# Delta-rule attention and a gelu MLP in one kernel: another list for the order of all five engines

## The chip, the cores and the metric

The kernel runs on one core of a Trainium2 chip. The core has a matmul engine (TensorE, PE in the profile; its weight loads are listed as PEld), a vector engine (VectorE, DVE), an engine for activation functions (ScalarE, ACT), a general engine (GpSimd, POOL), and SyncE (SP), which here only issues DMAs. ACT and POOL issue some DMAs too. Each engine works through its own row of instructions in order; waits between engines are waits on semaphores. PE reads operands from SBUF and writes into PSUM, which has eight banks.

The metric is the device time of one execution in microseconds (us); less is better.

## The reference

Two computations in a row. First a delta-rule attention over 4 batches, 8 heads, 768 positions and a head size of 48:

```python
k_n = k / (np.linalg.norm(k, axis=-1, keepdims=True) + 1e-06)
state = zeros((B, H, D, D))
for t in range(S):
    y[:, :, t] = einsum('bhd,bhde->bhe', q[:, :, t], state)
    v_old = einsum('bhde,bhd->bhe', state, k_n[:, :, t])
    state = state + beta_t * einsum('bhd,bhe->bhde', k_n[:, :, t], v[:, :, t] - v_old)
```

Its output, 3072 tokens of 384 numbers (8 heads of 48), goes through an MLP: `h = x @ w_in` (384 to 2048), gelu in its tanh form, `g @ w_out` (2048 to 384).

## The kernel before

**Attention.** The 768 positions are cut into 12 chunks of 64, c0 to c11. All 32 batch-head pairs are worked on together. Within a chunk the recurrence becomes matrices of 64 by 64: the keys of a chunk are normalized (`sq`, the square; `ss`, its sum; `sr` and `nw`, the root by two ways; `rn`, the reciprocal; `Kn`, the normalized keys), the keys and queries are turned by PE (`KQT` holds the result), products of keys with keys are formed (the "own" products of 32 by 32 blocks, and `G`, `Tt`, `DT` from the larger ones), a triangular system is solved, and from the solution come the factors (`Yf`, `tmp`, `XW`, `TB`, `WB`, `DI`, `ET`, `TT`) of an inverse. With it the chunk's `R` (values less what the state predicts), `U` (the solved values), the new state `S` and the output `x` are made. State follows state: c1 needs c0's.

Chunks 0 and 1 are solved singly: chunk 0's solve runs on DVE (lines 799 to 832), chunk 1's on POOL. From chunk 2 on they are solved in pairs, on POOL: 28 short instructions on `Yf` and `tmp` (L790, L793) between the transposition `Tt` on DVE that opens the solve (L904) and `XW` that ends it (L840, L846). Copies of `TB` by DMA (SP's queue) and expansions (`WB`, `DI`, L1024) follow, then PE's inverse.

The norm of chunks 0 to 5 takes its root on ACT; that of c6 to c11 is computed without ACT's root, by three rounds of short instructions that go to and fro between DVE and POOL (L633 to L644, the parts marked `norms(..., True)` on POOL), for two chunks at once.

**MLP.** Tokens come in 8 tiles: t0 to t3 are chunks 0 to 3 (64 positions of 4 batches, so 256 columns), t4 to t7 are two chunks each (512 columns). The first layer (`x,W` in the profile) has 16 blocks of 128, each followed by gelu on ACT (`gT`); the second (`W,gT`) sums over them and is copied out through `osb`.

**Order.** The program first records every operation with its reads and writes (`Plan.op`), and numbers it. Nothing is planned at build time beyond that: `Plan.schedule` (lines 137 to 166) reads a long string, `ORDER`, from left to right. A token is a letter for the engine (p, v, a, g, s for PE, DVE, ACT, POOL, SP) and the number of an operation; each engine's row is its tokens in that order. So a token can also say on which engine an operation runs, where several can do it. A token `wK.B` is K matmuls on a constant of zeros, `wz`, into bank B of PSUM (`spin`, line 415; the matmuls appear as L418 with `ps<-wz`): they compute nothing that is used. A second string, `BANK`, gives the PSUM bank of every result of PE. `Plan.emit` then puts the waits: an operation waits for what it reads, for the readers of what it overwrites, and for the last users of the bank that it takes.

## Time and profile before

| | |
|---|---|
| three runs | 244.82 us median (242.86 to 246.46) |
| profiled execution | 245.22 us |
| its span, from first to last instruction | 243.4 us |
| mean granted clock of PE | 0.958 of full |
| busy: PE, PEld, DVE, ACT, POOL | 221.4, 149.5, 157.4, 148.9, 123.3 us |

The span is what the profiler sees between the first and the last instruction; the 1.8 us between it and the execution's time lie around it. PE is busy for 91% of the span. PE's busy time counts the matmuls on the constant, and a matmul at half clock counts with its longer duration. In the rows of a timeline, the first number is the start in us from the span's start, the second the length, then engine, line, operation, what is written from what is read, and the count; in brackets stands how long the engine had been idle and what ended that. Line numbers are those of the kernel before; the changed kernel has one line more at the head, so that all of its numbers below are higher by one.

### The profile page before, as it was taken

The numbers are of one execution on the slowest core, as the hardware profiler recorded it, in microseconds if no ns is written. First come the engines' busy times: TensorE is split into PE (matmuls) and PEld (weight loads), VectorE is DVE, ScalarE is ACT, GpSimd is POOL, SyncE is SP. The second block draws the span as 40 slices with busy tenths as digits, with TensorE's granted clock in tenths as the row PEclk, the third lists the DMA queues.
The fourth block names the chain that finished last, engine by engine and source line by source line (L and its number), as shares of the span: only waits on it lengthen the run. The fifth ranks groups of instructions, "written<-read, shape, count | busy, mean of one in ns | idle before, by whom it ended". The sixth has DMA issues, their size and how long they took to land.

```text
span 243.4 us, 11359 instructions
## 1 busy us (share of the span) xinstructions
PE 221.4 (91%) x5084; PEld 149.5 (61%) x5102; DVE 157.4 (65%) x317; ACT 148.9 (61%) x295; POOL 123.3 (51%) x261
## 2 busy tenths in 40 slices
PE   7778867978896999999997999998899999999995
PEld 4354546767575976878874676565556656555562
DVE  6689984969797558985998988688736562000000
ACT  2247833688787477954976788735596437635502
POOL 4249897698588861888736886568700000000000
PEclk9999965799999589999999999999999999999999
DMA  6999999999645334575226311352032311200113
GB/s 140 180 156 162 187 198 131 198 180 159 114 86 112 81 74 98 97 163 97 41 67 159 67 37 38 73 101 74 3 62 59 60 39 47 72 33 32 64 35 129
DMA packets 64785, 23.78 MB, mean 98 GB/s; under 512 B 53600, under 2 KB 63840, under 8 KB 64736
## 3 DMA queue, kind: packets, MB, share of 16 engines
q1 hardware_dynamic: 57952, 14.66, 34.7%
q10 hardware_dynamic: 5728, 5.25, 7.5%
q0 software_dynamic: 1056, 3.15, 7.5%
q8 instruction: 40, 0.66, 1.2%
q14 instruction: 9, 0.07, 0.1%
HBM read 20.64 MB, written 4.72 MB: 104 GB/s over the span
## 4 chain that ended last, share of the span: by engine, by line
PE 59%; DMA 13%; ACT 8%; DVE 7%; SPq 4%; POOL 3%; issue 3%; ACTq 1%
PE ps L268 57%; DMA kf<-in_k_dram 12%; SPq L276 4%; ACT G L261 2%; DMA x<-x 1%; DVE TT L1131 1%; ACTq L276 1%; PE ps L663 1%; ACT gT L261 1%; DVE DT L750 1%; ACT sq L261 1%; ACT ET L1090 1%; POOL tmp L790 1%; ACT Tt L740 1%; POOL Yf L793 1%
## 5 line engine op out<-in xcount | busy, mean ns | idle before, releaser
L268 PE MATMUL ps<-x,W 128*128 128x256 bf16 (+1 forms) x369 | 68.9, 335 | 3.8 <-issue 1.4
L261 ACT ACTIVATE gT<-ps 128x512 bf16<-128x512 f32 x96 | 53.2, 605 | 30.0 <-PE ps L268 28.1
L268 PE MATMUL ps<-W,gT 128*128 128x384 bf16 x384 | 67.3, 327 | 0.2 <-issue 0.2
L268 PEld LDWEIGHTS ps<-x,W 128*128 128x128 bf16 x384 | 41.2, 117 | 21.6 <-DVE DT L750 2.1
L268 PEld LDWEIGHTS ps<-W,gT 128*128 128x128 bf16 x384 | 35.9, 98 | 23.3 <-issue 0.3
L793 POOL TENSOR_TENSOR Yf<-Yf,tmp 128x28 f32<-128x28 f32 (+13 forms) x84 | 30.2, 360 | 6.4
L790 POOL TENSOR_TENSOR tmp<-Yf 128x28 f32<-128x28 f32 (+13 forms) x84 | 30.1, 359 | 5.9
L257 DVE COPY osb<-ps 128x384 f32<-128x384 f32 x8 | 4.4, 554 | 29.5 <-PE ps L268 29.5
L1131 DVE TENSOR_TENSOR TT<-ps,DI 64x384 bf16<-64x384 f32 (+5 forms) x36 | 15.2, 422 | 7.1 <-PE ps L268 6.7
L1024 POOL TENSOR_TENSOR DI<-TB,mB 128x384 bf16<-128x384 bf16 x12 | 11.0, 933 | 16.3 <-DMA TB<-TB 13.8
L750 DVE TENSOR_TENSOR DT<-ps,mD 128x512 bf16<-128x512 f32 x24 | 15.9, 683 | 4.8 <-ACT G L261 4.8
L418 PE MATMUL ps<-wz 128*128 128x512 bf16 x69 | 17.1, 402 | 1.7 <-DVE pat L425 1.3
L261 ACT ACTIVATE osb<-ps 128x384 f32<-128x384 f32 x16 | 7.7, 488 | 16.5 <-PE ps L268 13.7
L252 DVE TENSOR_TENSOR TT<-ps,DI 128x768 bf16<-128x768 f32 (+2 forms) x18 | 12.1, 684 | 8.7 <-PE ps L268 8.6
L261 ACT ACTIVATE G<-ps 128x512 bf16<-128x512 f32 x24 | 13.6, 592 | 2.4 <-DVE Tt L742 1.4
L261 ACT ACTIVATE x<-ps 128x1024 bf16<-128x1024 f32 (+3 forms) x14 | 11.3, 824 | 5.6 <-PE ps L268 5.6
L268 PE MATMUL ps<-KQT 48*64 48x128 bf16 (+1 forms) x640 | 11.9, 208 | 2.9 <-ACT KQT L261 1.4
L261 ACT ACTIVATE sq<-kf 128x768 f32<-128x768 f32 (+1 forms) x11 | 8.9, 813 | 8.4 <-DMA kf<-in_k_dram 8.3
L611 DVE TENSOR_REDUCE ss<-sq 128x16 f32<-128x768 f32 (+1 forms) x13 | 11.3, 879 | 3.3 <-ACT sq L261 3.3
L268 PEld LDWEIGHTS ps<-TT,ET 64*64 64x64 bf16 x640 | 10.3, 113 | 4.4 <-issue 1.5
L418 PEld LDWEIGHTS ps<-wz 128*128 128x128 bf16 x72 | 7.1, 103 | 9.4 <-DVE pat L425 1.3
L268 PEld LDWEIGHTS ps<-KQT 48*64 48x64 bf16 (+1 forms) x640 | 8.7, 101 | 6.2 <-ACT KQT L261 2.3
(146 smaller groups left out, 363.7 us busy)
## 6 DMA issues: line engine op xcount, KB each, us to landing
qf<-in_q_dram SPq DMA_DIRECT2D x24, 192.0 KB, 4.5
kf<-in_k_dram SPq DMA_DIRECT2D x23, 192.0 KB, 5.6
vf<-in_v_dram SPq DMA_DIRECT2D x40, 96.0 KB, 3.3
out_dram<-osb ACTq DMA_DIRECT2D x16, 192.0 KB, 2.1
W<-in_moe_w_out_dram POOLq DMA_DIRECT2D x4, 384.0 KB, 8.9
out_dram<-osb ACTq DMA_DIRECT2D x16, 96.0 KB, 3.1
vf<-in_v_dram SPq DMA_DIRECT2D x4, 192.0 KB, 5.8
W<-in_moe_w_in_dram POOLq DMA_DIRECT2D x2, 384.0 KB, 9.5
```

The source lines that it names most:

```text
L252: return lambda e: e.tensor_tensor(out() if callable(out) else out, a() if callable(a) else a, b() if callable(b) else b, op)
L257: return lambda e: e.tensor_copy(out, a() if callable(a) else a)
L261: return lambda e: e.activation(out, a() if callable(a) else a, func)
L268: ins = t.matmul(out, lhsT, rhs, start=st, stop=sp_, skip_group_check=skip)
L276: return lambda e: e.dma_start(out, a)
L418: ins = e.matmul(psum[:, b, :], wz[:, 0:128], wz[:, :], start=True, stop=True)
L611: fr = lambda e, u=u: e.tensor_reduce(ss[j][:, u], sq[:, u, :], AX.X, ALU.add)
L750: op(d_ps(512), {"dve": lambda e: e.tensor_tensor(dv, gview(1)(), md, ALU.mult)}, reads=[h] + MD, writes=[dn])
L790: sop(nb * s * w, lambda e, s=s, w=w, tv=tv: e.tensor_tensor(tv, yf[:, :, s:s + 1, 0:s].to_broadcast([128, nb, w, s]), Yv()[:, :, s + 1:16 ...
L793: sop(nb * s * w, lambda e, s=s, tv=tv: e.tensor_tensor(Yv()[:, :, s + 1:16, 0:s], Yv()[:, :, s + 1:16, 0:s], tv, ALU.add), [YN, TN], [YN])
L1024: return e.tensor_tensor(o_.rearrange("q p (b j) -> q p b j", j=16), i_.unsqueeze(2).to_broadcast([128, n_, 3, 16]), mB[:, 16 - 16 * w:64 ...
L1131: ins = e.tensor_tensor(TT[r_][o_, par::2, cols], bank(hk, par)[i_, 0:8 * n].rearrange("q (p t) -> q p t", t=n), DI[r_][o_, par::2, 16 * k ...
```

## The change

Both strings are replaced as a whole; nothing else is touched. All operations are the same, apart from the matmuls on the constant: six tokens with 72 such matmuls became one with five. The table itself tells a reader nothing, so that only these pieces are shown:

```diff
 ORDER = """
-v0 g11 s52 a53 g21 v37 v5 v49 w6.0 g22 a51 s50 g16 v6 g18 v8 v38 v44 g13 v4 v1 s57 a2 g14 g12 g19 v15 s58 v48 g20 v39
...
+g405 w5.3 g406 v254 s119 g407 s118 a221 g35 v304 s116 g408 s117 g409 p314 s114 g410 a378 g411 p231 s266 a309 g412 v379
...
-BANK = ("06035030223020716021312502331474655413667456202312530375435460212600502436647540243530466307732633"
+BANK = ("0070325215530761467526743765467223026600550166045677331475733026221446304255770173061702204601200627"
```

What this does to the rows is shown at three places. The first is the start. PE's first row before, in which `wz` marks the matmuls on the constant, `Kn` the turning of keys, `KQT 32x32` an own product of a chunk and `DI`, `WB` the inverse of chunk 0:

```order
L418 MATMUL ps<-wz 128x512 x6
L268 MATMUL ps<-identF,gT 128x128 x3
L418 MATMUL ps<-wz 128x512 x22
L695 MATMUL ps<-identB,Kn 128x128 x8
L268 MATMUL ps<-KQT 32x32 x64
L418 MATMUL ps<-wz 128x512 x12
L663 MATMUL ps<-identB,Qn 128x4x2x16 x16
L695 MATMUL ps<-identB,Kn 128x128 x8
L268 MATMUL ps<-KQT 32x32 x64
L268 MATMUL ps<-KQT 64x128 x32
L418 MATMUL ps<-wz 128x512 x29
L268 MATMUL ps<-R,TT 64x48 x16
```

and PE's row now, from the same place on:

```order
L269 MATMUL ps<-identF,gT 128x128 x3
L696 MATMUL ps<-identB,Kn 128x128 x8
L269 MATMUL ps<-KQT 32x32 x64
L696 MATMUL ps<-identB,Kn 128x128 x8
L269 MATMUL ps<-KQT 32x32 x64
L664 MATMUL ps<-identB,Qn 128x4x2x16 x16
L269 MATMUL ps<-KQT 64x128 x32
L269 MATMUL ps<-TT,G 64x48 x32
L269 MATMUL ps<-R,TT 64x48 x16
L696 MATMUL ps<-identB,Kn 128x128 x16
L269 MATMUL ps<-DI,ET 64x48 x16
L269 MATMUL ps<-KQT 32x32 x64
```

The constant's matmuls are gone from here; the five that are left stand ahead of the first state product of chunk 1 and of the MLP's first group. The keys of chunks 2 and 3 are turned earlier (`Kn`, 16 matmuls), and the own products of these two chunks, which stood behind chunk 0's state, stand inside chunk 0's inverse.

The second place is ACT. Its row near the start before, where `warm` is a one-element root whose only use is to bring a table of functions in early:

```order
L261 ACT_TABLE_LOAD
L261 ACTIVATE warm<-warm 128x1
L261 ACTIVATE sq<-kf 128x384
L455 ACTIVATE mF<-me 64x48
L261 ACTIVATE sr<-ss 128x16
```

and now:

```order
L262 ACT_TABLE_LOAD
L262 ACTIVATE sq<-kf 128x384
L262 ACT_TABLE_LOAD
L262 ACTIVATE warm<-warm 128x1
L262 ACTIVATE sr<-ss 128x16
```

The square of chunk 0's first half has moved ahead of `warm`, and the program has a third load of a table (the other one stands ahead of the first gelu in both). Further down in ACT's row the square of chunk 4's keys, which before stood between the copies of the inverse of chunk 0 (`WB`) and its `U`, stands behind chunk 0's `S` and ahead of the last copy of `x`; on DVE its sum moves likewise. DVE takes chunk 1's `Kn` from POOL and does it ahead of chunk 0's solve, has two sums inside that solve where it had one, and has the `Kn` of chunks 2 and 3 ahead of the first `ET` of chunk 0's factors. Two copies of `KQT` that stood inside that solve are ACT's now.

The third place is the solve of chunks 6 and 7. DVE's row before, from the last part of the key products (`Tt1`) on; `Tt0` is the transposition that opens the solve, `rn` the reciprocal of the norms of chunks 8 and 9, `Kn2` the keys of chunk 8:

```order
L742 SCALAR_TENSOR_TENSOR Tt1<-ps,mH,Tt1 128x2x128
L750 TENSOR_TENSOR DT3<-ps,mD 128x2x4x64 x2
L904 STREAM_TRANSPOSE Tt0<-Tt1 128x1024
L637 SCALAR_TENSOR_TENSOR nw<-nw,sr 128x32
L638 SCALAR_TENSOR_TENSOR sr<-nw,sr 128x32
L252 TENSOR_TENSOR TT1<-ps,DI1 128x16x48
L252 TENSOR_TENSOR S0<-ps,S1 128x16x48
L257 COPY KQT2<-ps 128x2x4x128
L257 COPY KQT3<-ps 128x2x4x128
L252 TENSOR_TENSOR R0<-ps,vf1 128x768
L252 TENSOR_TENSOR ET1<-ps,mE 128x2x8x48
L252 TENSOR_TENSOR TT1<-ps,DI1 128x16x32
```

and now, where `rn` stands ahead of the last two parts of `Tt1` and of `Tt0`:

```order
L638 SCALAR_TENSOR_TENSOR nw<-nw,sr 128x32
L639 SCALAR_TENSOR_TENSOR sr<-nw,sr 128x32
L751 TENSOR_TENSOR DT3<-ps,mD 128x2x4x64
L751 TENSOR_TENSOR DT2<-ps,mD 128x2x4x64
L642 TENSOR_SCALAR nw<-nw 128x32
L645 RECIPROCAL rn<-nw 128x32
L736 TENSOR_SCALAR Tt1<-ps,mH 128x2x128
L743 SCALAR_TENSOR_TENSOR Tt1<-ps,mH,Tt1 128x2x128
L905 STREAM_TRANSPOSE Tt0<-Tt1 128x1024
```

POOL's row ahead of the same solve, whose first instruction is `Yf0<-Tt0,bM0`, before:

```order
L1024 TENSOR_TENSOR DI1<-TB0,mB 128x8x48
L257 CAST Qn<-qf 128x2x8x48
L1024 TENSOR_TENSOR DI1<-TB0,mB 128x8x48
L1024 TENSOR_TENSOR DI2<-TB0,mB 128x8x48
L257 CAST Qn<-qf 128x2x8x48
L252 TENSOR_TENSOR nw<-sr,ss 128x32
L252 TENSOR_TENSOR bM0<-nbT,mS 128x512
L252 TENSOR_TENSOR nw<-sr,ss 128x32
L252 TENSOR_TENSOR Yf0<-Tt0,bM0 128x512
```

and now:

```order
L1025 TENSOR_TENSOR DI2<-TB0,mB 128x8x48
L253 TENSOR_TENSOR nw<-sr,ss 128x32 x2
L1025 TENSOR_TENSOR DI1<-TB0,mB 128x8x48 x2
L253 TENSOR_TENSOR nw<-sr,ss 128x32 x2
L258 CAST Qn<-qf 128x2x8x48 x2
L253 TENSOR_TENSOR Kn3<-kf0,rn 128x16x48
L253 TENSOR_TENSOR Kn2<-kf2,rn 128x16x48
L253 TENSOR_TENSOR Yf0<-Tt0,bM0 128x512
```

Two `Kn` that were DVE's are POOL's here, ahead of the solve, and the last two steps `nw` of the norm stand behind all expansions `DI` of chunks 4 and 5's factors. On PE the first product that needs this solve's result (`WB` of chunk 7) stands some ten operations earlier in its row.

More of the change, by code (lines that the diff above doesn't have):

```diff
@@ L76 @@
[L76 to L81 removed]
+s52 v45 a53 g13 v48 g11 g16 s50 v4 a51 v36 v37 v5 g18 s55 g12 g21 v15 g14 s54 g19 g20 g22 p64 s57 v66 s59 v8 v49 a85
@@ new lines @@
+p599 a597 s261 p244 v600 g813 v598 a601 v572 p341 a602 g214 p452 p342 a337 a453 v573 v603 p343 g574 a245 p344 g456
+v454 p345 p441 v575 g439 a346 v347 p604 a442 v576 p609 v605 g577 p356 g614 v578 v579 a606 v610 p360 s226 v580 v611
+a607 p364 g457 v581 a612 v582 v615 p248 a514 g515 s524 s525 p249 a361 g583 v608 s223 a357 g616 a365 v613 s225 p443
+a584 a458 v585 p459 g617 v444 a250 s522 p362 g618 a460 s224 g619 p366 v586 g620 p339 a367 p445 g621 v340 a440 g622
+p587 s593 a689 g623 v446 p467 g624 p461 a363 v468 g625 p447 a588 g626 g627 p354 v448 v462 g628 p469 a355 g629 p352
```

111 lines of the change are left out of this document (53 added, 58 removed).

## The prediction

> **What bounds the kernel now.** I read the page of the profile first, then its windows by stage, then the chain of waits, and last the timelines of single engines.
>
> ```profile
> span 243.4 us, 11359 instructions
> PEclk9999965799999589999999999999999999999999
> L418 PE MATMUL ps<-wz 128*128 128x512 bf16 x69 | 17.1, 402 | 1.7 <-DVE pat L425 1.3
> ...
> 20.00:42.60 22.60, 17.73 (x467) 11.87 (x458) 17.78 (x40) 12.90 (x33) 19.41 (x45) 0.78 1.08 171
> 42.60:60.00 17.40, 15.29 (x330) 12.36 (x332) 14.49 (x23) 13.88 (x28) 14.35 (x30) 0.90 1.07 178
> 60.00:80.00 20.00, 17.22 (x494) 13.06 (x495) 16.25 (x34) 15.41 (x35) 15.54 (x31) 1.00 0.60 113
> 80.00:88.00 8.00, 8.00 (x226) 6.72 (x223) 3.49 (x6) 4.41 (x6) 6.92 (x18) 0.57 0.19 39
> 80.30:87.10 6.80, 6.80 (x212) 5.85 (x212) 3.19 (x6) 3.85 (x5) 5.72 (x17) 0.50 0.18 35
> 88.00:122.00 34.00, 33.67 (x956) 26.21 (x956) 28.55 (x50) 24.56 (x46) 21.89 (x42) 1.00 0.52 102
> 133.00:202.00 69.00, 66.16 (x1985) 42.53 (x1993) 49.59 (x90) 44.67 (x84) 31.91 (x71) 1.00 0.26 56
> 202.00:243.40 41.40, 38.20 (x216) 21.63 (x209) 2.90 (x4) 18.11 (x34) 0.00 (x0) 1.00 0.18 61
> ```
>
> The rows of windows give the stretch, its length, and the busy time of PE, PEld, DVE, ACT and POOL, then the clock. There are two regimes. From 88 us on PE is busy for nearly the whole stretch (33.67 of 34.00, 66.16 of 69.00): nothing but fewer or shorter PE instructions, or a new wait, changes the time there. Before 88 us there is slack: PE idles 2.1 us in 42.6 to 60 and 2.8 us in 60 to 80, and ran 6.8 us from 80.3 at a clock of 0.50. Before 42.6 us 17.1 us of its busy time are matmuls on the constant, so PE waits for the chain of chunk 0 there:
>
> ```profile
> 15.80 1.57 POOL Kn L252
> ...
> 18.03 15.39 DMA kf<-in_k_dram
> 33.45 0.85 ACT sq L261
> 34.32 0.95 DVE ss L611
> 35.27 0.60 DVE DT L750
> 35.87 0.60 DVE KQT L257
> 36.47 0.47 DVE U L257
> ```
>
> Each row is start, length, what. A load of k for a later chunk lands at 33.4; its square stands ahead of chunk 0's work in ACT's row, its sum in DVE's, so chunk 0's U comes only at 36.47.
>
> **The first 45 us.** The numbers needed:
>
> ```profile
> 2.15 1.28 ACT L261 ACT_TABLE_LOAD   x1 [2.15 <-issue]
> 7.89 0.52 ACT L261 ACTIVATE sq<-kf 128x384 f32<-128x384 f32 x1 [4.25 <-DMA kf<-in_k_dram]
> 9.50 0.22 ACT L261 ACTIVATE sr<-ss 128x16 f32<-128x16 f32 x1 [0.95 <-DVE ss L611]
> 22.74 0.95 DVE L611 TENSOR_REDUCE ss<-sq 128x16 f32<-128x768 f32 x1
> 31.84 1.01 DVE L252 TENSOR_TENSOR Kn<-kf,rn 128x768 bf16<-128x768 f32 x1
> 12.90 0.65 PE L268 MATMUL ps<-KQT 48*32 48x32 bf16 x64 [1.15 <-ACT KQT L261]
> 36.99 0.53 PE L268 MATMUL ps<-U,Kn 64*48 64x48 bf16 x32 [2.02 <-DVE U L257]
> 41.09 1.36 PE L268 MATMUL ps<-KQT 48*32 48x32 bf16 x128
> 42.44 1.44 PE L268 MATMUL ps<-x,W 128*128 128x256 bf16 x6
> 74.75 1.50 PE L268 MATMUL ps<-x,W 128*128 128x256 bf16 x12
> ```
>
> *Constant matmuls removed.* 67 of 72 go. Each group stood in a gap in which PE had to wait for chunk 0, so I take 0 for their time. What they held up is the clock: it was full from 5 to 32.5 us. That is worth little there: 64 small matmuls took 0.65 us at full clock (12.90), 128 took 1.36 at half (41.09). For the MLP's large ones it is worth nearly half (1.44 us for six at 42.44, 1.50 for twelve at 74.75), but the clock was at half when these began, spins or not. Cost 0, bounds 0 and 2 (eighteen large ones more at half clock, 0.115 each).
>
> The Trainium skill, "TensorE: Matmul & The Clock Gate", Part 1, says that the clock falls to half after an idle window of about 3.4 us, whatever ran before, and rises after one busy window. By that rule five matmuls just ahead of the MLP warm nothing and the first MLP groups run at half clock, as they did in this trace; it would leave the sum as it is unless gaps between those groups come back, which is a rival below.
>
> *Second table load.* The row now has sq ahead of warm, with a load before each. The first falls into the wait for k; the second begins when sq ends: 8.41 + 1.28 + 0.20 for warm = 9.89, where sr began at 9.50: +0.4 us. Other reordered rows around it (the sum and the beta transposition on DVE) I put at up to 0.6; the first own product moves from 12.9 to 13.9: +1.0.
>
> The Trainium skill, "ScalarE: Activation LUTs", section "What ACT_TABLE_LOAD costs", puts a drain of about 1.4 us on every switch of set beside 1.28 us of load. The load's 1.28 is in this trace; no row shows a drain. With it, this step would be an estimated +1.8 in place of +0.4.
>
> *DVE and ACT ahead of chunk 0's factors.* DVE takes chunk 1's Kn from POOL (1.57 there, 1.01 here), ahead of the solve of chunk 0: +1.0. Two sums instead of one stand inside that solve: +0.95. Two Kn of chunks 2 and 3 stand ahead of the factors' ET: +2.0. Two KQT copies leave that stretch for ACT: -1.2. One square (0.85) now stands on ACT ahead of the last copy of x, which gives the MLP its input: +0.85. And the square and sum that held up U are behind it: PE's wait of 2.02 us at 36.99 goes. Sum with the start: 1.0 + 1.0 + 0.95 + 2.0 + 0.85 - 1.2 - 2.0 = **+2.6**: the first MLP group at 45.0 instead of 42.4. Bounds: -1 (the additions fill gaps of DVE, which is busy 17.78 of 22.60 us) and +6 (the copies hold ACT up too).
>
> **From 45 to 88 us.** What waits here are the states of chunks 2 and 3, whose solve as a pair on POOL is late:
>
> ```profile
> 42.52 1.25 DVE L904 STREAM_TRANSPOSE Tt<-ps 128x1024 f32<-128x1024 f32 x1 [1.47 <-PE ps L268]
> 62.49 1.21 POOL L846 TENSOR_TENSOR XW<-Yf,nbT 128x256 bf16<-128x256 f32 x2
> 79.08 0.24 PE L268 MATMUL ps<-DI,ET 64*64 64x48 bf16 x4 [1.02 <-issue]
> ```
>
> The own products of chunks 2 and 3 stand now ahead of chunk 0's inverse on PE, not behind its state, and the transposition that opens the solve can run at about 37 us instead of 42.5. POOL still has chunk 1's solve to end, so I take 4 us earlier; two casts of Q (0.8 each) move out of it too, and XW is done at about 57, not 63.7. Then the inverses and states of this pair need not be waited for: PE's slack of 2.1 + 2.8 us and the cold stretch can go. At half clock 6.8 us cost between 0 (all small matmuls) and 3.4 (all large); the stretch is mixed: 2.0. Sum 6.9, of which I leave 0.3 for a Q cast that now comes late: **-6.6**, bounds 0 and -8. So at 88 us PE is ahead by 6.6 - 2.6 = 4.0 us.
>
> **From 88 to 133 us.** This lead meets the solve of chunks 6 and 7:
>
> ```profile
> 100.89 1.97 DVE L904 STREAM_TRANSPOSE Tt<-Tt 128x1024 f32<-128x1024 f32 x1
> 103.24 0.26 POOL L252 TENSOR_TENSOR nw<-sr,ss 128x32 f32<-128x32 f32 x1 [0.66 <-DVE sr L638]
> 103.45 1.28 POOL L252 TENSOR_TENSOR Yf<-Tt,bM 128x512 f32<-128x512 f32 x1
> 109.45 0.34 DVE L644 RECIPROCAL rn<-nw 128x32 f32<-128x32 f32 x1
> 119.21 1.21 POOL L846 TENSOR_TENSOR XW<-Yf,nbT 128x256 bf16<-128x256 f32 x2
> 121.87 0.84 PE L268 MATMUL ps<-x,W 128*128 128x256 bf16 x6
> 122.75 0.53 DVE L1024 TENSOR_TENSOR WB<-TB,mB 128x768 bf16<-128x768 bf16 x1
> 129.11 0.44 PE L268 MATMUL ps<-WB,G 64*64 64x48 bf16 x32
> 132.20 1.24 PE L268 MATMUL ps<-x,W 128*128 128x512 bf16 x5 [1.25 <-ACT ET L1090]
> ```
>
> From Tt at 100.89 to WB of chunk 7, ready at 123.3, runs an unbroken chain of POOL: 17 us. Before, PE asked for chunk 7's WB at 129.1, long after. The new list asks earlier: what stands ahead of that product now had been done in this trace at about 121.5, and with a lead of 4.0 PE is there at 117.5. The solve cannot move up as far. In DVE's row the reciprocal rn of chunks 8 and 9, at 109.45 in this trace and behind Tt, now stands ahead of Tt, and on POOL two Kn of these chunks (1.57 each by the row at 15.80) stand ahead of Yf; the two Kn run beside Tt and its last addends (some 3.2 us), so they cost nothing if rn comes in time. With all of it I put Tt, and so WB, at 2.1 us earlier than before: 121.2. PE then waits 3.7 us, and the lead left is **-0.3**. Bounds: WB as late as now, 123.3, makes +1.8; a WB that keeps step with PE makes -4.0.
>
> **After that.** The wait at 132.2 stays: in SP's row the moves of x for the next tile now stand some 1.5 us later behind TB's copies, but PE has just waited, so 0, bounds -1.2 and +1.5. From 133 us the same matmuls are in another order behind one another; PE's 2.8 us of idle there, and 3.2 in the last stretch, most of it the tail, I leave: 0, bounds -2 and +1.
>
> **Sum.** +2.6 - 6.6 + 3.7 + 0 = -0.3 against the profiled run of 245.22 us (span 243.4, 1.8 outside it): 244.9. That run lies 0.4 over the median of 244.82, so the time to expect is **244.5 us**.
>
> **Rivals.**
>
> *Faster: the lead survives.* If pair 6 and 7 keeps step (bound -4.0) and half of the later start isn't there (1.3 less), the profiled run becomes 245.2 - 5.3 = 239.9 and the median 239.5; with all of it, 238.2. For it speaks that before 88 us PE has the 6.9 us of slack worked out above, and that all of the start's additions lie on DVE and ACT, which had gaps. Against it: the 17 us of solve that don't shrink, and a list in which PE wants their result 10 operations sooner. The windows from 88 us on say that a lead is kept only if no wait is put into PE's work; here one is.
>
> *Slower: rn holds up Tt.* The norm of chunks 8 and 9 goes to and fro between DVE and POOL; its last POOL step ended at 103.5, and on POOL it stands now behind two expansions of DI, which wait for a copy of TB by DMA. If that step comes no earlier than 103.5, then rn (0.34), two parts of Tt and the transposition of 1.97 end at about 107, WB at 127, and PE, due at 121.5 without a lead, has lost 5.5: 250.7 in the profiled run, 250.3 as a median. It decides from the point where the last nw is later than about 102. Against it: the copies of TB for chunks 4 and 5 come earlier when PE is ahead.
>
> *Slower: the MLP stays at half clock.* If PE's gaps after 45 us come back at each group, the 48 matmuls of the first tile's first layer cost 0.24 us instead of 0.125 each. That is 5.5 us, of which this trace already pays 2.0 for its first eighteen: 3.5 more than in the sum, 248.0, within 2%.
>
> *No change at all.* From 88 us PE does the same work. If gains and losses ahead of it cancel, the time is as before, 244.8; my sum is nearly that case, and I count it there.
>
> **Chances.** About 2% is what a measurement of this kernel can tell from no change: 239.9 and 249.7. My forecast with its near neighbours (no change; the half-clock MLP, most of it) 0.51; the lead surviving 0.26; rn or a start 6 us later, unrecovered (251 at worst), 0.23. So faster 0.26, same 0.51, slower 0.23. The range reaches into both rivals: from 238.2, the whole lead, to 250.3; the likeliest case alone spans 241 to 248.
>
> **What would show it.** Right: the ACT row shows two loads ahead of sr, and sr at about 9.9; the first x,W group at 44 to 47 us; XW of pair 2 and 3 at about 57; no half clock at 80 to 87; PE some 4 us ahead at 88 and a wait of 2 to 5 us for WB of chunk 7 near 118. Wrong: no such wait (then faster), the last nw of chunks 8 and 9 after 102 us (then slower), or a start later than 48.

## The result, and the profile after

The changed kernel takes **264.81 us** (median of four runs, 264.23 to 265.19); the kernel before, run beside it, 245.05. The ratio is 1.081 (95% interval 1.073 to 1.090): slower by 8%, outside the forecast range of 238.2 to 250.3. Ratios here leave out executions that are 1.5% or more longer than the fastest of their kernel, medians don't.

The runs below were made in five further sets, each with the kernel before beside it; its median went from 242.4 to 245.6 us from set to set. Kernels of different sets are therefore compared by their ratios to the kernel before, and a difference of 2 or 3 us between their times alone says little.

The page of the changed kernel, its span and two rows of its 40 slices (busy tenths of PE, granted clock):

```profile
span 262.8 us, 11239 instructions
...
PE   2132475698988789798979899999997989999995
...
PEclk9999999999999977999999999999999999999999
```

Windows of the changed kernel (stretch, length, busy PE, PEld, DVE, ACT, POOL, then the clock):

```profile
20.00:42.60 22.60, 11.63 (x329) 9.44 (x329) 15.69 (x40) 13.21 (x32) 18.81 (x44) 1.00 1.13 177
42.60:60.00 17.40, 13.09 (x238) 9.57 (x239) 9.54 (x15) 11.53 (x27) 13.84 (x35) 1.00 0.53 78
88.00:122.00 34.00, 29.00 (x791) 23.15 (x791) 24.79 (x42) 19.66 (x35) 20.91 (x42) 0.90 0.43 87
133.00:202.00 69.00, 66.40 (x1612) 41.58 (x1603) 49.59 (x89) 45.06 (x84) 36.56 (x77) 1.00 0.32 68
```

PE issued 329 matmuls in 20 to 42.6 us where it had issued 467, and idled 5.0 of the 34 us from 88 us on, where it had idled 0.33. The clock of 1.00 in the first rows is not to be trusted: the clock was first recorded at 57.2 us, and the matmuls ahead of it have the pace of half clock (of the 18 `x,W` at 54.06 below, the first 15 start 0.21 us apart, the last 0.11).

The waits of PE in the changed kernel (what waited, for whom, us in total, times, longest):

```profile
PE ps L269 <- issue: 9.3, 8, 2.3
PE ps L696 <- DVE Kn L253: 7.6, 2, 5.9
PE ps L269 <- DMA x<-x: 4.8, 4, 1.5
PE ps L664 <- ACT Qn L262: 4.6, 1, 4.6
```

The same view of the kernel before begins with this row:

```profile
PE ps L268 <- issue: 2.9, 11, 1.0
```

"issue" is time in which PE waited for nothing that the profile shows. Nine of the eleven stops of before, 0.15 to 0.18 us each and 1.5 us together, lie inside rows of large matmuls; that trace holds 5084 matmuls for 5102 weight loads, so these are most likely matmuls whose records are missing. The changed kernel's trace holds 5035 of both and has no such stops. Without them, and with a stop of 1.0 us that the view lists under L696, PE stopped for 1.3 us before (two stops) and for 10.3 us now (nine). The timeline of the changed kernel has the other places:

```profile
6.45 1.28 ACT L262 ACT_TABLE_LOAD   x1 [6.45 <-DMA kf<-in_k_dram]
7.74 0.52 ACT L262 ACTIVATE sq<-kf 128x384 f32<-128x384 f32 x1
8.28 1.28 ACT L262 ACT_TABLE_LOAD   x1
9.58 0.20 ACT L262 ACTIVATE warm<-warm 128x1 f32<-128x1 f32 x1
9.69 0.20 ACT L262 ACTIVATE sr<-ss 128x16 f32<-128x16 f32 x1
...
13.67 1.25 POOL L253 TENSOR_TENSOR bM<-btz,mS 128x512 f32<-128x512 f32 x1 [5.28 <-DVE btz L253]
13.79 1.96 DVE L253 TENSOR_TENSOR Kn<-kf,rn 128x768 bf16<-128x768 f32 x1
...
28.12 0.63 DVE L838 STREAM_TRANSPOSE TB<-XW 128x256 f32<-128x256 f32 x1
...
38.07 0.41 PE L269 MATMUL ps<-R,TT 64*64 64x48 bf16 x7 [1.82 <-issue]
44.54 0.53 PE L269 MATMUL ps<-KQT 48*64 48x128 bf16 x11 [2.30 <-issue]
...
51.26 2.31 PE L419 MATMUL ps<-wz 128*128 128x512 bf16 x5 [1.18 <-DVE osb L1224]
54.06 3.68 PE L269 MATMUL ps<-x,W 128*128 128x256 bf16 x18
```

Chunk 0 is solved (`TB`) 3.0 us later than before (25.13), the first MLP group begins at 54.06, 11.6 us later. From there to the end of one group of tile 2's first layer, which the trace puts at 104.4 us before and at 116.7 now, the distance is nearly the same. From that group to the span's end it is 146.1 against 139.0: another 7.1 us. So some 12 of the 19.4 us are lost ahead of the MLP, 7 in its second half, nothing between. In that second half PE waits 3.3 us for x and stops for 2.8 us at "issue", where it was 0.5 and 0.3 before.

**Where the "issue" stops lie.** The DMA view lists a queue of the kind "instruction". From its records and the rows of matmuls, I counted the matmul at which each of these stops lies:

```
kernel    packet of 16384 bytes: asked, ended   PE stopped ... went on   at matmul no.
before            76.43   77.82                  78.05 ... 79.08          1493 = 11*128 + 85
after             35.62   36.60                  36.25 ... 38.07           351 =  2*128 + 95
after             41.44   43.02                  42.24 ... 44.54           479 =  3*128 + 95
after             90.69   91.64                  91.29 ... 92.96          1498 = 11*128 + 90
after            130.39  131.50                 131.45 ... 132.85         2519 = 19*128 + 87
```

They lie whole multiples of 128 matmuls apart (the remainder falls slowly, since PE's row holds 34 semaphore instructions too and before's trace lacks 18 matmuls), and each ends 1.3 to 1.5 us after a packet has. I call these places marks. PE went on 2.3 to 3.1 us after the packet had been asked for, and it had been asked for only 0.6 to 1.6 us before PE stopped; what sets the moment of the asking is not shown. 128 matmuls and their 128 weight loads are 256 instructions. The Trainium skill, "Runtime: NRT & Kernel Launch", section "Instruction fetch mechanics", says that an engine's instructions come in blocks of 16 KiB, which are 256 instructions, and that crossing a block's end is mostly hidden. The first half agrees with these records; the second does not agree with stops of up to 2.3 us.

### The profile page after: what moved, and what is told of

Same layout as the page of the kernel before. It is cut to its first block, busy times and chain, and to the rows that moved or that the text cites. A ratio compares the mean times of both kernels' runs of the same rounds, so it can differ in the third digit from the quotient of the medians.

```text
span 262.8 us, 11239 instructions
## 1 busy us (share of the span) xinstructions
PE 214.7 (82%) x5035; PEld 146.8 (56%) x5035; DVE 165.5 (63%) x312; ACT 154.3 (59%) x302; POOL 121.3 (46%) x260
## 4 chain that ended last, share of the span: by engine, by line
PE 58%; DVE 12%; ACT 9%; DMA 7%; SPq 6%; issue 6%; ACTq 0%
PE ps L269 55%; SPq L277 6%; DMA x<-x 4%; DMA kf<-in_k_dram 2%; DVE Kn L253 2%; PE ps L664 1%; DMA TB<-TB 1%; ACT KQT L262 1%; PE ps L696 1%; ACT L262 1%; ACT x L262 1%; PE ps L419 1%; ACT Qn L262 1%; ACT G L262 1%; DVE R L253 1%
## 5 line engine op out<-in xcount | busy, mean ns | idle before, releaser
L269 PE MATMUL ps<-x,W 128*128 128x256 bf16 (+1 forms) x384 | 72.3, 336 | 5.0 <-DMA x<-x 4.8
L791 POOL TENSOR_TENSOR tmp<-Yf 128x28 f32<-128x28 f32 (+13 forms) x84 | 27.9, 332 | 6.3
L269 PE MATMUL ps<-KQT 48*64 48x128 bf16 (+1 forms) x640 | 13.8, 220 | 8.7 <-ACT KQT L262 4.5
L1025 POOL TENSOR_TENSOR DI<-TB,mB 128x384 bf16<-128x384 bf16 x12 | 11.6, 979 | 19.4 <-DMA TB<-TB 13.5
L262 ACT ACTIVATE KQT<-ps 128x1024 bf16<-128x1024 bf16 (+1 forms) x15 | 14.4, 966 | 9.1 <-PE ps L696 7.3
L262 ACT ACTIVATE x<-ps 128x1024 bf16<-128x1024 f32 (+2 forms) x15 | 11.0, 731 | 12.5 <-PE ps L269 11.3
L269 PEld LDWEIGHTS ps<-KQT 48*64 48x64 bf16 (+1 forms) x640 | 9.6, 108 | 12.9 <-ACT KQT L262 5.3
L696 PE MATMUL ps<-identB,Kn 128*128 128x128 bf16 x96 | 9.1, 250 | 8.6 <-DVE Kn L253 7.6
L253 DVE TENSOR_TENSOR R<-ps,vf 128x768 bf16<-128x768 f32 x11 | 10.5, 956 | 8.5 <-PE ps L269 8.5
L253 DVE TENSOR_TENSOR S<-ps,S 128x768 bf16<-128x768 f32 x10 | 9.6, 956 | 9.1 <-PE ps L269 9.0
L262 ACT ACTIVATE osb<-ps 128x384 f32<-128x384 f32 x15 | 7.4, 491 | 13.3 <-PE ps L269 11.2
L253 DVE TENSOR_TENSOR TT<-ps,DI 128x768 bf16<-128x768 f32 (+2 forms) x18 | 12.1, 680 | 2.9 <-PE ps L269 2.8
L696 PEld LDWEIGHTS ps<-identB,Kn 128*128 128x128 bf16 x96 | 6.9, 112 | 9.6 <-DVE Kn L253 8.0
```

The lines of the kernel that those rows point to most:

```text
L253: return lambda e: e.tensor_tensor(out() if callable(out) else out, a() if callable(a) else a, b() if callable(b) else b, op)
L262: return lambda e: e.activation(out, a() if callable(a) else a, func)
L269: ins = t.matmul(out, lhsT, rhs, start=st, stop=sp_, skip_group_check=skip)
L696: ins = e.transpose(tb()[:, m, :], t[:, 2 * m:2 * m + 2, :].rearrange("p h d -> p (h d)"), identB[:, :])
L791: sop(nb * s * w, lambda e, s=s, w=w, tv=tv: e.tensor_tensor(tv, yf[:, :, s:s + 1, 0:s].to_broadcast([128, nb, w, s]), Yv()[:, :, s + 1:16 ...
L1025: return e.tensor_tensor(o_.rearrange("q p (b j) -> q p b j", j=16), i_.unsqueeze(2).to_broadcast([128, n_, 3, 16]), mB[:, 16 - 16 * w:64 ...
```

## The experiments

Eighteen kernels were run. The diffs show one engine's tokens of `ORDER`, with those of the other engines left out.

### What the constant matmuls are worth

**b_nospin**: the kernel before without its 72.

```diff
-w6.0 p64 w10.5 w12.1 p96 p94 p155 w12.1 p102 p103 p112 p267 p182 p179 w29.7 p192 p187 p302 p194 w3.0
+p64 p96 p94 p155 p102 p103 p112 p267 p182 p179 p192 p187 p302 p194
```

> The kernel before without its 72 matmuls on the constant, nothing else changed. Theory clock: PE stays at half clock until the MLP runs, the first MLP group starts 3 to 5 us later than at 42.4, time 247 to 251. Theory order: the matmuls on the constant are worth nothing, time 243 to 246.

Measured: 253.74 us (253.10 to 259.69), 1.050 of before (1.044 to 1.056). One edit that the prediction had at 0 costs 5%, some 12 us, more than either theory had. Its waits and its first MLP group:

```profile
PE ps L269 <- issue: 8.4, 8, 2.2
...
PE ps L269 <- DMA x<-x: 1.9, 2, 1.6
```

```profile
45.78 1.44 PE L269 MATMUL ps<-x,W 128*128 128x256 bf16 x6
```

The group begins 3.3 us later, but six matmuls take 1.44 us as before: the MLP began at half clock in both. And from tile 2's group on the same order takes 142.3 us to the last matmul where it took 136.0, though no constant was ever there: PE stops for 3.0 us at "issue" there (0.3 before) and waits 1.9 us for x (0.5 before).

**a_warm** and **a_warm2**: 67 put back into the changed kernel's gaps (in a_warm one group took a PSUM bank that chunk 0's solve needed; on DVE the zeros of `wz` are written earlier).

```diff
-p64 p94 p96 p155 p112 p267 p102 p103 p182 p179 p187
+w6.1 p64 w20.1 p94 p96 p155 w6.6 p112 p267 w18.6 p102 p103 w8.2 p182 p179 w9.2 p187
```

> The changed order with 67 matmuls on the constant put back into PE's gaps of the first 31 us (6 at the start, 20, 6, 18, 8 and 9 between the first steps of chunks 0 and 1), banks and all other rows unchanged. Theory clock: without these matmuls PE ran at half clock until the MLP had begun (57 us), and each PE step on chunk 0's chain was longer by it; then the first MLP group starts 3 to 6 us earlier than at 54.1, the turning of 16 keys takes 1.2 us in place of 1.9, and the time is 258 to 262. Theory order: what is late is DVE's and ACT's rows; then the first MLP group comes within 1 us of 54.1 and the time is 263 to 266. Theory instruction supply: the two stalls of 1.8 and 2.3 us in front of the MLP, which lie 128 matmuls apart, move with the number of matmuls issued, and stay 128 apart.

> The changed order with the 67 matmuls on the constant put back at the same six places as in a_warm, now in banks that nobody needs soon (in a_warm those behind chunk 1's own product held a bank that DVE's solve of chunk 0 waited for, 4.9 us). Theory clock: with PE at full clock from about 6 us on and no wait for a bank, the first MLP group comes 3 to 6 us earlier than at 54.1 and the time is 257 to 262. Theory order: within 1 us of 54.1, 263 to 266.

Measured: 268.60 (267.59 to 270.67) and 265.66 (264.70 to 266.53): 1.114 (1.106 to 1.122) and 1.088 (1.083 to 1.093) of before, nothing gained. The "issue" waits of a_warm2 are 12.1 us, 10.1 without the short ones, one of them 4.9. The clock was not kept up: in a_warm2 its records have it at full from 6.4 us, but at half from 13.3 to 23.5 and from 37.2 to 57.6. So these runs show that 67 constants at these places bring nothing; what a clock that stays full would bring to this order they don't show.

**b_phase** and **b_ns72** take the two things that a constant matmul does apart: it takes time (and keeps PE warm), and it counts. The forms of 64x48 are a second branch in `spin`; in the tokens below, a number above 100 stands for its last two digits of them.

```diff
 b_phase, from the kernel before
-w29.7
+w21.7 w164.7
 b_ns72, from b_nospin
-p182 p179 p192
+p182 p179 w172.7 p192
```

> The kernel before, its row of 29 spins (at 20.3 to 26.5 us, while TensorE waits for chunk 0's factor) made 21 spins and 64 matmuls of 64x48, which is about the same time: 128 matmuls on the constant in all in place of 72, so that the marks at which TensorE's row of instructions is refilled (every 128 matmuls) fall on the real products where they fell in the run named b_nospin. Theory P (where these marks fall decides the 6 us by which b_nospin was longer from tile 2's products on, 142.3 against 136.0 us with the same order): first MLP group at 42 to 44 us as before, the stretch from tile 2 on 141 to 143 us, time 248 to 252. Theory C (those 6 us come from being 2 to 3 us late and from the clock, not from the marks): 135 to 137 us and 243 to 247.

> The run named b_nospin with 72 matmuls of 64x48 on the constant in the gap at 20.4 to 26.9 us: the marks fall as in the kernel before, without the time of its spins. Theory P: first MLP group at 45 to 46 us, the stretch from tile 2 on 135 to 137 us, time 246 to 249. Theory C: 141 to 143 us, time 252 to 255.

Measured: b_phase 256.68 us (253.05 to 261.61), 1.050 (1.041 to 1.059); b_ns72 **244.37** (242.29 to 250.23), 1.000 (0.995 to 1.006). b_phase, in its waits and timeline:

```profile
PE ps L269 <- issue: 10.0, 17, 1.8
PE ps L269 <- DVE U L258: 8.4, 1, 8.4
```

```profile
40.91 0.84 ACT L262 ACTIVATE sq<-kf 128x768 f32<-128x768 f32 x1 [8.85 <-DMA kf<-in_k_dram]
```

b_ns72, in its waits and timeline:

```profile
PE ps L269 <- issue: 2.6, 11, 0.6
```

```profile
26.77 0.62 PE L269 MATMUL ps<-R,TT 64*64 64x48 bf16 x16 [2.16 <-DVE TT L937]
...
43.45 1.44 PE L269 MATMUL ps<-x,W 128*128 128x256 bf16 x6
```

Together:

| constant matmuls | time, of before | "issue" waits | without those under 0.2 us | tile 2's group to the last matmul |
|---|---|---|---|---|
| 72 wide (before) | 1 | 2.9 us | 1.3 us | 136.0 us |
| none (b_nospin) | 1.050 | 8.4 us | 8.4 us | 142.3 us |
| 64 wide, 64 narrow = 128 (b_phase) | 1.050 | 10.0 us | 8.4 us | 141.6 us |
| 72 narrow (b_ns72) | 1.000 | 2.6 us | 1.0 us | 135.0 us |

0 and 128 put every mark on the same real matmul, and both are slow; 72 is fast, wide or narrow. The stops of b_nospin (first row) and b_phase (second row) do come at the same matmuls:

```profile
45.49 0.27 PE L269 MATMUL ps<-KQT 48*32 48x32 bf16 x18 [2.23 <-issue]
51.35 0.27 PE L269 MATMUL ps<-KQT 48*32 48x32 bf16 x18 [1.69 <-issue]
```

So do those ahead of the last 20 `DT,U` of a group (2.25 us in b_nospin, at 86.75; 1.75 in b_phase, at 92.12). b_ns72 has no wide one left, its narrow ones ran 0.053 us apart, the pace of half clock (in b_phase, at full clock, 0.032), and its `R,TT` at 26.77 took 0.62 us, where the kernel before needed 0.43 for the same 16. So what the 72 are worth is their count, which sets where the marks fall; their clock is worth nothing that shows here. b_phase holds a second loss that has nothing to do with the marks: the keys of chunk 4 landed at 40.9 us in its profile, not at 33.4, and U stood behind their sum (8.4 us). That load stands at the same place in SP's row; why it landed late isn't shown, nor in what share of b_phase's runs it did (the profiled one took 256.94 us, the fastest 253.05). So its 12 us are marks and this load together. The last column lies behind that load: of the 5.6 us there, stops at marks are 2.7 (3.0 against 0.3) and waits for x 0.7 (1.2 against 0.5).

**b_tail**: 768 narrow ones behind the last operation of the kernel before, to measure a dense row by itself (here the token's number is the count).

```diff
-(the last token)
+(the last token) w768.2
```

> The kernel before with 768 small matmuls on the constant (64 by 64, 48 columns) in one unbroken row behind PE's last matmul; nothing waits for them but the end of the kernel. Theory instruction supply: each 128 matmuls are one 16 KB packet of instructions, and a packet takes some 4 us when the next is asked for right behind it: the tail takes 20 to 25 us, with a stop of 2 to 3 us at every 128th matmul. Rival: PE issues them as fast as inside the kernel, 32 in 0.39 us: 9.4 us.

```profile
251.87 38.91 PE L420 MATMUL ps<-wz 64*64 64x48 bf16 x768
```

The whole took 286.57 us (two runs, 280.07 and 293.07). But in the trace the 768 start one behind the other with no stop at any mark: the first hundred 0.032 us apart, the others 0.053, which is 6.8 us for 128. The window shows why these are slow:

```profile
251.00:290.00 39.00, 39.00 (x763) 38.49 (x762) 0.00 (x0) 0.49 (x1) 0.00 (x0) 0.55 0.07 23
```

The clock fell to half at 255.2 us. So this run measured narrow matmuls at half clock and not the packets; it shows only that packets keep up with one mark in 6.8 us. The long stops above lie in rows of small matmuls that are faster: at full clock 64 of the own products took 0.65 us.

### Single parts of the new order

**a_tab**: `warm` ahead of the first square again.

```diff
-a53 a51 a85 a2 a89 a90
+a53 a51 a2 a85 a89 a90
```

> The changed order with the one-element root (and the clearing of its operand) back ahead of the square of chunk 0's keys, so that there is one table load less and the first one needs no k. Theory: the load stood on the path, because it is issued behind the wait for k and not in it; sq starts 1.3 us earlier and sr 2.0 to 2.6 us earlier than at 9.7, and the time falls by 1 to 2.6 us, to 262 to 264. Rival: chunk 0 waits for something else, same time within 0.5 us.

Measured: 263.45 us (260.51 to 265.29), 1.087 of before (1.077 to 1.097). The root `sr` is 0.9 us earlier, not the 2.0 to 2.6 expected; against the changed kernel's 1.081 no gain is shown.

**a_sp**: SP's row so that loads which are ready stand ahead of the moves of x for tiles 2 to 4 that aren't. Six tokens further on in the row move forward as well.

```diff
-s484 s521 s348 s481 s483 s350 s520 s650 s649 s482 s485 s523 s476
+s521 s348 s350 s520 s484 s481 s483 s482 s485 s650 s649 s542 s543 s544 s541 s523 s476
```

> The changed order with SP's row alone changed: loads of q and v that were ready at 82 to 88 us go ahead of the moves of x for tile 2, and the moves of x for tiles 2, 3 and 4 stand together. Theory SP: PE's waits for x of tiles 2, 3 and 4 (1.5, 1.4 and 1.0 us) go, time 260.5 to 262. Rival: PE meets the next late input instead, time 263 to 265.

Measured: 262.33 us (260.46 to 263.15), 1.086 of before (1.076 to 1.095). PE's waits for x fall from 4.8 to 0.6 us, but the time is not shown to be less than the changed kernel's (1.081): it is 2.5 us lower, and so was the kernel before in this set (242.44 against 245.05). In the changed kernel SP's row around the second move reads:

```profile
99.95 0.69 SPq L277 DMA_DIRECT2D x<-x  x1
100.69 0.59 SPq L277 DMA_DIRECT2D qf<-in_q_dram  x1
101.32 0.62 SPq L277 DMA_DIRECT2D vf<-in_v_dram  x1
101.98 2.44 SPq L277 DMA_DIRECT2D x<-x  x2
104.47 0.64 SPq L277 DMA_DIRECT2D vf<-in_v_dram  x1
105.15 0.62 SPq L277 DMA_DIRECT2D qf<-in_q_dram  x1
```

The first move waits for x, the loads behind it wait with it, and then the later moves stand behind these loads, 0.6 us for each.

**a_start**, **a_head** and **b_loads**. a_start puts the rows of DVE, ACT and POOL up to chunk 0's `TT` back, and PE's turning of Q ahead of chunk 1's keys (`warm` stands as in a_tab with it). a_head is a_start with SP's first 14 loads put back as well; b_loads is b_nospin with the changed kernel's order of these loads and nothing else.

```diff
 a_start, of DVE
-v45 v48 v4 v36 v37 v5 v15 v66 v8 v49 v65 v1 v3 v70 v88 v86 v43 v67 v91 v92 v93 v107
+v0 v37 v5 v49 v6 v8 v38 v44 v4 v1 v15 v48 v39 v46 v47 v3 v10 v40 v36 v66 v65 v67 v86 v88
...
 a_head, of SP beside it (b_loads: the other way round)
-s52 s50 s55 s54 s57 s59 s60 s56 s62 s63 s58 s98 s99 s61
+s52 s50 s57 s58 s55 s54 s56 s59 s62 s61 s98 s63 s99 s60
```

> The changed kernel with the start of three rows put back as it was, up to the solved chunk 0: VectorE (up to TT), ScalarE (up to the other TT), GpSimd (with Kn of chunk 1), and TensorE's Q-transposes ahead of chunk 1's K-transpose; no spins are put back but the five that it has. Theory A (the start's order costs 3 us up to the solved chunk 0 and about 1.5 more through Q and TT): chunk 0 solved at 25.8 us in place of 28.8, TT at 27 in place of 31.2, U at 43 to 44, time 260 to 262. Theory B (the instruction supply sets the end of this stretch): TT is early, but PE's stalls between 128-matmul marks grow by what is gained, the first MLP group stays within 1.5 us of 54.1, time 263 to 265.

> The changed kernel with the run named a_start's edit and, beside it, SyncE's first 14 loads in the order of before (in a_start q of chunk 0 still landed at 17 us, its fourth part being eleventh in the row, and VectorE's solve waited for a product behind it, so that chunk 0 was solved no earlier). The stretch behind it keeps its order, with the two groups of 64 products among those of chunk 0. Theory A (what is late is made up to the solved chunk 0): q lands at 13 us, chunk 0 solved at 26, U at 43 to 44 and the first MLP group at 50 to 51, time 260 to 262. Theory B (the stretch is held by its own order and by instruction packets): chunk 0 solved at 26, but the first MLP group at 53 or later, time 263 to 265.

> The run named b_nospin (the kernel before without its spins) with SyncE's first 14 loads in the changed kernel's order, nothing else. Theory A (the late q is one of the causes): q at 17 us, the copies of Q 3 to 4 us later, chunk 1's own product behind them in TensorE's row late by as much, the solve of chunk 0 on VectorE waits for it, time 2 to 4 us over b_nospin's 253.7. Theory B (there is slack, since k of chunk 1 lands 2 us earlier): within 1 us of 253.7.

Measured: a_start 264.09 us (262.07 to 265.55), 1.083 of before (1.069 to 1.096); a_head **259.54** (258.54 to 261.60), 1.069 (1.059 to 1.080); b_loads 260.04 (257.00 to 261.05), 1.065 (1.054 to 1.077), against b_nospin's 1.050. The first fence below is a_start's timeline, the second a_head's, the third b_loads'; the first row of each is ACT's copy of Q, the second the end of chunk 0's solve, the third the first MLP group:

```profile
16.98 0.84 ACT L262 ACTIVATE Qn<-qf 128x768 bf16<-128x768 f32 x1 [3.80 <-DMA qf<-in_q_dram]
...
28.12 0.63 DVE L838 STREAM_TRANSPOSE TB<-XW 128x256 f32<-128x256 f32 x1
...
53.68 3.25 PE L269 MATMUL ps<-x,W 128*128 128x256 bf16 x18
```

```profile
13.09 0.83 ACT L262 ACTIVATE Qn<-qf 128x768 bf16<-128x768 f32 x1
...
25.56 0.63 DVE L838 STREAM_TRANSPOSE TB<-XW 128x256 f32<-128x256 f32 x1
...
51.08 3.23 PE L269 MATMUL ps<-x,W 128*128 128x256 bf16 x18
```

```profile
17.66 0.84 ACT L262 ACTIVATE Qn<-qf 128x768 bf16<-128x768 f32 x1 [5.14 <-DMA qf<-in_q_dram]
...
28.57 0.63 DVE L838 STREAM_TRANSPOSE TB<-XW 128x256 f32<-128x256 f32 x1
...
49.20 1.44 PE L269 MATMUL ps<-x,W 128*128 128x256 bf16 x6
```

One of the four loads of chunk 0's Q stands fourth in the row of before and eleventh in the new one, and Q lands at 17 us, not 13. With the rows of before that holds up the copy of Q, behind it chunk 1's own product on PE, and with it chunk 0's solve, since DVE's row has a step on that product inside the solve. All the row moves of a_start without it bring nothing (1.083 against 1.081). With it chunk 0 is solved and the MLP begun 2.6 us earlier, and the time falls by 1.3%, some 3 us; in the kernel before the same swap makes the MLP start 3.4 us later and costs 1.5%, some 4 us, as theory A of b_loads had it. The intervals of each pair still touch, so the new order of 14 loads is worth some 3 to 4 us by two pairs that agree, not by one that is clear. In a_head chunk 0 is solved when it was before (25.56 against 25.13), and yet the MLP begins 8.6 us later: most of what is lost ahead of the MLP lies between these two points.

**a_pe**: the turning of keys of chunks 2 and 3 and their own products behind chunk 0's inverse again, with what follows from them on DVE and ACT.

```diff
-p187 p189 p192 p126 p134 p196 p391 p194 p392 p198 p206 p203 p204 p302 p305 p210 p200 p201 p207 p211 p218 p219 p215 p220
+p187 p189 p192 p196 p194 p198 p206 p203 p204 p302 p305 p210 p200 p201 p207 p211 p126 p134 p218 p219 p215 p220 p391 p392
```

> The changed kernel with one stretch of TensorE's row put back as it was: the two K-transposes of chunks 2 and 3 and the two groups of 64 small products on their keys come behind chunk 0's products (the casts and copies that follow them are moved with them), as before the change; nothing else. Theory A (the order of this stretch holds chunk 0's chain, and these 32 + 128 extra matmuls use up two instruction packets in it): U of chunk 0, at 47.4 us in the changed kernel, comes 4 to 5 us earlier, the first MLP group at 49 to 51 us in place of 54.1, time 258 to 261. Theory B (the chain of chunk 0 is late because its factors and Q are late, TT at 31.2 and the copies of Q at 28.3): at most 1.5 us earlier, time 263 to 265.

Measured: 270.98 us (269.81 to 274.99), 1.111 of before (1.091 to 1.132), a miss to the wrong side. PE's waits of a_pe between 42 and 80 us:

```profile
PE ps L664 <- POOL Qn L258: 4.8, 1, 4.8
PE ps L269 <- issue: 4.0, 1, 4.0
```

Chunk 0's state did come earlier (its `U,Kn` at 44.6, not 49.0), but a stop of 4.0 us, ahead of the own products at 50.4, ate that before the MLP began, at 54.07 as ever. Then the solve of chunks 2 and 3 is late on POOL, and the changed row has tile 1's cast of Q behind it: 4.8 us more.

**a_mend** and **a_mend_sp**: a_pe, a_start and a_sp at once, without the five spins, and the same with 73 put back in the start.

```diff
-p64 p94 p96 p155 p112 p267 p102 p103 p182 p179 p187 p189 p192 p126 p134 p196
+p64 p94 p96 p155 p102 p103 p112 p267 p182 p179 p187 p189 p192 p196
 a_mend_sp, from a_mend
-p64 p94 p96 p155 p102 p103 p112 p267 p182 p179 p187 p189 p192 p196 p194
+w6.1 p64 w10.1 w12.1 p94 p96 p155 w13.6 p102 p103 p112 p267 p182 p179 w29.2 p187 p189 p192 p196 p194 w3.2
```

> Both of the two edits, the row of loads of the run named a_sp, and the five spins ahead of the first MLP group left out (nothing on a constant is left). If the costs add up as the two kernels with exchanged starts say (8 us of start, 3 of the rest, 9 to 11 of spins): about the time of the kernel before without its spins, 252 to 256, first MLP group at 45 to 47 us. If the rest of the changed order costs by itself: 258 or more.

> As the run named a_mend, with 73 matmuls on the constant put back at the five places of the start where the kernel before had them. If the spins are worth 9 to 11 us in the right places, as in the kernel before: 243 to 248, first MLP group at 42 to 43.5 us, and the clock full from 6 us but for the pauses. If their worth hangs on more than the start (the run named a_warm2, where they brought nothing): 251 to 256.

Measured: 271.26 (269.60 to 271.76) and 268.67 (267.47 to 269.12), 1.111 and 1.101 of before, far over every time expected but the open "258 or more". Both have a_pe's wait for the cast of Q, 4.6 and 4.7 us long, so they tell little of the sum.

### Exchanged halves

**h_astart** has the changed rows up to the first MLP group and the rest of before; **h_bstart** the other way round; **h_bstart2** is that with two rows mended (a sum on DVE and a load on SP move with them), **h_bns** the same without spins.

```diff
 h_bstart: of all five rows
-(after, up to p231)
+(before, up to p231)
 h_bstart2, of ACT and POOL beside it
-a253 a306 a212 a216 a221
+a306 a212 a216 a221 a253
-g403 g404 ... g418 g137 g419
+g403 g137 g404 ... g418 g419
```

> All rows up to the first MLP matmul as before, everything behind it in the order of the changed list, banks to match. If the two halves add up: the first MLP group at 42.4 us as before, and the rest as much longer than before as it was in the changed kernel (7.8 us): 251 to 254. If the rest was late only because the start was: 244 to 247.

> All rows up to the first MLP matmul as changed, everything behind it in the order of before. If the two halves add up: the first MLP group at 54.1, then as fast as before: 255 to 258. If the start's lateness is partly made good or the rest's loss comes from the start: under 252, or over 261.

> The rows of the kernel before up to the first MLP group (its spins among them), and from there the rows of the changed kernel, as in the run named h_bstart, but with the two rows mended that did not fit there: the square and the sum of chunk 4's keys come behind chunk 0's state (they stood ahead of U and waited for a load that landed at 41 us), and GpSimd's cast of tile 1's Q stands early in the solve of chunks 2 and 3, as before (it stood near the solve's end). Theory A (nearly all of the 20 us is made ahead of the first MLP group; the rest costs the 3 us by which the changed kernel is over the run named h_astart): first MLP group at 42 to 44 us, time 245 to 250. Theory B (the changed order of the rest is slower by itself wherever it starts from): first MLP group as early, time 254 or more.

> The run named h_bstart2 without its 72 spins. Theory A: first MLP group at 45 to 47 us as in the run named b_nospin, time 254 to 258. Theory B: 262 or more. If the spins are worth less with this rest than the 9 to 11 us that they were worth in the kernel before, the two runs lie within 5 us of each other.

Measured: h_astart 262.00 us (261.52 to 264.55), h_bstart 266.77 (263.02 to 268.09), h_bstart2 263.98 (262.44 to 265.19), h_bns 265.64 (263.48 to 266.29); of before 1.075, 1.083, 1.085 and 1.091. Either half alone costs nearly all of the 20 us, so these don't add. What h_bns shows is why:

```profile
64.70 0.85 PE L269 MATMUL ps<-DI,identB 64*64 64x384 bf16 x4 [4.99 <-DVE DT L751]
```

The changed row of DVE puts the end of the solve of chunks 2 and 3 ahead of a `DT` that PE wants, which is right only where that solve began early, as it does in the changed start. The list is one piece; halves of it meet waits that neither list has. These four runs bound nothing, and I draw nothing else from them.

## Why the prediction was wrong

**The step that failed is "Constant matmuls removed ... Cost 0, bounds 0 and 2".** It asked what these matmuls take and what they warm, and found both to be next to nothing. The runs agree: b_ns72 does without the wide ones and without their clock, and its MLP begins at half clock as the kernel before's does. But they also count. Without them the kernel before takes 5% more, some 12 us, and 72 narrow ones, which warm nothing that shows, take that back (1.000). The prediction's own fence had the row that could have led there, `79.08 ... [1.02 <-issue]`; I used it as a time and didn't ask what "issue" was. The rule of the Trainium skill that is cited there ("TensorE: Matmul & The Clock Gate", Part 1), that the clock falls to half after an idle window of about 3.4 us, does not fit all of these traces: in the kernel before it fell at 80.3 us, and in the 3.4 us ahead of that PE was busy for 1.9 and never idle for more than 1.02; in b_tail it fell behind 3.3 us of narrow matmuls without a gap. It bears on little of the time here.

How much of the changed kernel's 19.4 us comes through this is less sure. Its stops are 9.0 us more than before's (10.3 against 1.3). With 72 constants (a_warm2) they are 10.1 us and the kernel is no faster than with 5, so those two counts are both bad for this order; other counts weren't tried.

**"The first 45 us": +2.6, bounds -1 and +6; it was +11.6.**
- The start: `sr` at 9.69 us, forecast 9.89; the first own product at 13.4, forecast 13.9. The first load of a table doesn't fall into the wait for k, as the step had it: it stands behind that wait (6.45). The drain of 1.4 us that the Trainium skill, "ScalarE: Activation LUTs", section "What ACT_TABLE_LOAD costs", adds to a switch is in no row: the square ends at 8.26, the load runs from 8.28 to 9.56, and `warm` starts at 9.58.
- Chunk 1's `Kn` on DVE, put at 1.0, took 1.96 beside POOL's `bM`. Chunk 0's solve does end 3.0 us later (28.12), but with the rows of before it ends at 28.12 too (a_start); only with the order of the first loads put back does it end at 25.56 (a_head). That order isn't in the sum at all. The new rows with the old loads were not run, so what they cost by themselves isn't shown.
- U's wait of 2.02 us did go, and two stops of 1.82 and 2.30 us at marks, in the stretch that now holds 144 matmuls more, took its place. The five spins, which the step didn't price, waited 1.18 us for their bank and ran 2.31; without them PE could have begun the MLP at most 1.3 us earlier, since ACT's last copy of chunk 0's `x` ended at 52.7 us (argued, not run alone).
- "A start later than 48" was named as what would make the forecast wrong. It was, and it cost more than the 251 put on it there.

**"From 45 to 88 us": -6.6; it was about +0.7** up to tile 2's group. The solve did end at 57.4 us, forecast 57, and the half-clock stretch at 80 us went. But the slack was not PE's to keep: stops of 0.69, 1.05 and 1.67 us at marks (64, 87 and 91 us) and a wait of 1.49 us for x took it, and a half-clock stretch came back at 95 to 102.

**"From 88 to 133 us": +3.7** for WB of chunk 7, to eat a lead of 4.0. There was no lead, so no such wait, and the rival of the surviving lead went with it. Of the rival with rn the sign did come: the last `nw` ended at 113.8 us, and `Tt` began at 116.6, 15.7 us later than before, where PE at tile 2's group was 12.3 later. But its price did not: PE shows no wait for chunk 7's WB. The half-clock rival didn't come: of the first group's 18 only 15 ran at half clock, which the sum already held.

**"After that ... so 0, bounds -1.2 and +1.5"** for the moves of x was mis-sized: PE's waits for them are 4.8 us, against 0.5 before. What they cost in the end isn't shown: a_sp, in which they are 0.6 us, is not clearly faster. The step looked at TB's copies and missed the loads in the same row.

So the single edits put a price on one part, the order of the first loads, with some 3 to 4 us; for the moves of x and for the table they show no gain. The traces show 9.0 us more of stops at marks and 4.3 more of waits for x. These overlap (in b_loads the loads alone raised the stops from 8.4 to 10.0 us) and need not add, as a_mend and the halves showed. How the 19.4 us divide among them stays open. The new banks were not tried alone. No version beat the kernel before; the best of the changed order was a_head.

## What to carry to other kernels

- A matmul that computes nothing still takes its place in the row of instructions. Before adding or removing any, look at where "issue" stops lie, and count: 56 matmuls more in an idle gap cost 12 us here (some of it a late load), 72 narrow ones in place of none won as much. A fast list may be fast only for its own count, so compare orders at several.
- Read SP's row like any other engine's: a transfer that waits holds all behind it, and the order of the first fourteen loads was worth some 3 to 4 us.
- Compare kernels by their ratio to one that runs beside them. Two edits here look 1.4 and 2.5 us faster by their times; by their ratios no gain is shown.
- A list of orders is tuned as one piece. Undoing part of it made it worse three times (a_pe, a_mend, a_mend_sp), so test a part only with all that waits on it.

## What the runs showed of the hardware

- PE's instructions come by DMA in packets of 16384 bytes, 128 matmuls with their weight loads. In rows of small matmuls PE stops at such a mark until 1.2 to 1.6 us after a packet has ended, for up to 2.3 us in the changed kernel. The smallest distance between two askings was 3.2 us (b_nospin, 150.11 and 153.36); a row of narrow matmuls at 6.8 us per 128 had no stop (b_tail).
- The clock can fall while PE works: in b_tail it went to half at 255.2 us, behind 3.3 us in which narrow matmuls followed one another 0.032 us apart.
- The profile gives the clock as 1.00 ahead of its first record, here at 57 us, while matmuls had the pace of half clock.
- The keys of chunk 4, sent from the same place in SP's row, were there by 33.4 us in the kernel before and at 40.9 and 41.2 us in b_phase and h_bstart.
- DVE's `Kn` of 128x768 took 1.96 us beside POOL's `bM` and 2.24 beside POOL's own `Kn` (b_nospin, 32.42), 1.01 in the kernel before. POOL's `Kn` took 2.21 us there, 1.49 in the kernel before.
